# Attention and a two-layer MLP on one core: loads of later chunks with plain token order, K evacuated by two engines, zero fills moved, and product 1 of chunk 0 woven into chunk 1

## The chip, the core and the metric

The kernel runs on one NeuronCore of a Trainium2 chip. Its engines have instruction streams of their own: PE (matrix products and transposes; its weight loads are listed apart as PEld), DVE (vector), ACT (scalar, activation functions), POOL (GpSimd) and SP (which only issues transfers here). The data lie in HBM; SBUF is the working memory and PSUM the memory into which PE writes. The metric is device time in microseconds (us), lower is better. Three runs of the kernel before took 298.2, 299.79 and 300.01 us, the median is 299.79 us.

## The reference

Sliding-window and full attention for 4 batches, 8 heads, 768 tokens and head size 64, followed by two matrix products with a leaky ReLU between them:

```python
scores = scale * q @ k.T                       # per batch and head, 768 x 768
keep_stream = causal & (key < 4 | query - key < 64)
mask = causal if is_retrieval[h] else keep_stream   # heads 0, 2, 6 are retrieval heads
a = softmax(where(mask, scores, -1e9))
x = (a @ v).transpose(0, 2, 1, 3).reshape(3072, 512)
h = x @ w_in                                   # 512 -> 2048
out = maximum(0.01 * h, h) @ w_out             # 2048 -> 512, float32
```

All inputs are float32 in HBM; the products on PE are in bfloat16 with float32 sums.

## The kernel before

The 3072 tokens are eight chunks of 384 (`CH`), two per batch: chunk n is half c = n mod 2 of batch n div 2. Each chunk goes through five steps, and the order of all of them is written out by hand: every engine works through its own list in the order in which the Python code emits the calls, and semaphores make it wait for data.

- **load**: `load_chunk(n)` issues from SP the transfers of k, q and v of chunk n into float32 stage tiles `f` (four of them, used in turn). Token 3p+g of a chunk of q and k goes to partition p, slot g, so that 3 x 64 floats (768 bytes) lie in a row in HBM; one transfer carries all of k or of q. For v, token 128g+p goes to partition p, slot g, in three transfers with rows of 64 floats (256 bytes).
- **cast**: `cast_chunk(n)` turns them into bfloat16 on POOL (for chunk 0 DVE, ACT and POOL share this); `v_shift(n)` copies V, shifted by 64 tokens, into `vb` with two transfers issued from ACT.
- **prep**: `prep_slots(n)` has eight slots, K and Q in turn for four pairs of heads. A slot transposes three 128x128 blocks on PE into PSUM (`pt`, L213) and evacuates them: Q with one copy on DVE (L216), K with two copies of 64 partitions into `kt` (L224 on DVE; in chunks 0 and 1 the second is an ACT copy, L222). Since token 3p+g sits at column p of block g, the copies read PSUM with a step of 128 elements to put the tokens in order. The first four keys of the streaming heads are copied to `ksink` by POOL (L227). Two halves of one PSUM bank take turns as `pt`; in chunks 0 and 1 a third tile, `py`, joins them.
- **attention**: `attention_slots(n)` has units of scores (L296, L331), the exponential on ACT (L301, L336), a mask product on DVE (L305, L340) and, two slots later, the product with V (L251). One unit, `sink_qk`, makes the scores of the four sink keys from `ksink` (L268). A finished pair of heads is scaled on DVE (L357, L359), transposed on PE (L365) and copied by ACT to `xt` (L366). Half c = 1 has 26 slots, half c = 0 has 17 (chunk 0 among them).
- **products**: `in_slots(n)` has 16 ticks of four products (L419) with a leaky ReLU on ACT each (L421); `out_slots(n)` has 16 slots with 48 products (L433), three copies on DVE (L444) and three transfers from SP (L445).

`merge(ms, as_)` puts two lists of slots into one order, spread evenly. In the steady state the prep and attention slots of chunk n+1 are spread over the 32 product slots of chunks n and n-1. The start is different: chunk 0's prep and attention run alone; then come four ticks of product 1 of chunk 0, then prep of chunk 1, then ticks 4 to 11 merged with attention of chunk 1, then 20 ticks in a row (12 of chunk 1, the last four of chunk 0, the last four of chunk 1); then product 2 of chunk 0 merged with prep and attention of chunk 2.

At the very start POOL makes the constant masks, DVE copies some of them together (L117 to L125) and fills the unused halves of `kt` with zeros (L153, L154); after that the two halves of chunk 0's heads are cast and prepared one after the other (L477 to L489).

## Time and profile before

| | |
|---|---|
| median of three runs | 299.79 us |
| time of the profiled execution | 302.08 us |
| its span, first to last instruction | 300.3 us |
| PE busy | 252.7 us, 84% of the span |
| ACT busy | 140.8 us, 47% |
| DVE busy | 130.2 us, 43% |
| POOL busy | 55.6 us, 19% |
| transfers | 32.36 MB, 50760 packets |

How to read it: a row of the table of stages gives a stretch of time, then for each engine its busy time and its number of instructions, the clock that PE was granted (1.00 is full), the busy share of the transfer engines and the rate. A row of the timeline gives start, duration, engine, line, operation, output and input, a count, and in brackets how long the engine had been idle and which instruction or transfer ended that. A queue's name with a q (SPq, ACTq) is the engine that issues transfers; its time is that of the issuing. A row of a group gives count, busy time in us, and the mean of one in ns. PE's products are pipelined, so that the durations of products in a row overlap.

### The profile page before, as it was taken

To read this page: it belongs to the slowest core of one execution; us is meant where nothing else is said; L and a number is where in the kernel's file an instruction comes from. 1 tells how busy PE (TensorE), PEld (TensorE's weight loads), DVE (VectorE), ACT (ScalarE), POOL (GpSimd) and SP (SyncE) were. 2 spreads that over 40 slices of the span, in tenths; PEclk is the share of its full clock that TensorE was granted. 3 is DMA by queue.
4 is the path that set the end of the run, shared out by engine and by line. 5 is a ranking of instruction groups with operands and counts; after the bars stand their busy time and mean duration, and the time that the engine had idled before them with its cause. 6 is when DMAs were issued, how large, how long until landed. Compare 5 with 4: busy or idle time off the path is not lost.

```text
span 300.3 us, 5297 instructions
## 1 busy us (share of the span) xinstructions
PE 252.7 (84%) x2111; PEld 149.9 (50%) x2140; DVE 130.2 (43%) x304; ACT 140.8 (47%) x304; POOL 55.6 (19%) x121
## 2 busy tenths in 40 slices
PE   0266859879789879999999789998998799999994
PEld 0145435555436435665566446664664356655541
DVE  4665552420357563336654552436645623310011
ACT  2164337867305315773366337761565157633300
POOL 8449321000016006000340042000700000000000
PEclk9998577999959999999999999999999999999999
DMA  8899999930100198014901591109511110010011
GB/s 189 230 229 280 208 220 196 285 77 0 35 2 35 37 262 175 2 37 116 281 27 38 115 284 42 37 19 284 119 37 34 56 37 15 23 37 35 35 70 70
DMA packets 50760, 32.36 MB, mean 108 GB/s; under 512 B 26032, under 2 KB 46768, under 8 KB 50736
## 3 DMA queue, kind: packets, MB, share of 16 engines
q1 hardware_dynamic: 45088, 25.04, 31.7%
q0 software_dynamic: 4224, 4.19, 8.2%
q10 hardware_dynamic: 1424, 2.79, 4.3%
q8 instruction: 16, 0.26, 0.4%
q14 instruction: 8, 0.07, 0.1%
HBM read 27.26 MB, written 6.29 MB: 112 GB/s over the span
## 4 chain that ended last, share of the span: by engine, by line
PE 74%; DVE 16%; ACT 4%; issue 3%; POOL 1%; ACTq 0%; DVEq 0%; POOLq 0%
PE ph L419 25%; PE py L433 24%; DVE kt L224 8%; PE pt L213 6%; PE po L251 6%; PE psS L296 4%; PE pt L365 2%; PE psS L433 2%; PE psS L331 2%; DVE xs L359 2%; ACT at L301 1%; DVE o L444 1%; PE psS L268 1%; ACT kt L222 1%; DVE qt L216 1%
## 5 line engine op out<-in xcount | busy, mean ns | idle before, releaser
L419 PE MATMUL ph<-xt,w_in_bf 128*128 128x384 bf16 x512 | 104.5, 333 | 0.1
L421 ACT ACTIVATE g<-ph 128x384 bf16<-128x384 f32 x128 | 62.7, 490 | 83.0 <-PE ph L419 82.4
L433 PE MATMUL py<-w_out_bf,g 128*128 128x512 bf16 x324 | 91.5, 387 | 2.1 <-DVE o L444 0.4
L419 PEld LDWEIGHTS <-w_in_bf 128*128 128x128 bf16 x512 | 46.5, 99 | 29.2 <-issue 4.3
L301 ACT ACTIVATE at<-psS 128x384 bf16<-128x384 f32 x81 | 39.1, 490 | 24.0 <-PE psS L296 23.0
L433 PEld LDWEIGHTS <-g 128*128 128x128 bf16 x384 | 33.8, 98 | 25.2 <-issue 2.8
L224 DVE COPY kt<-pt 64x384 bf16<-64x384 bf16 x54 | 29.9, 554 | 30.7 <-PE pt L213 30.3
L305 DVE TENSOR_TENSOR at<-at,m_caus 128x128 bf16<-128x128 bf16 x72 | 18.1, 279 | 39.6 <-ACT at L301 39.4
L444 DVE COPY o<-py 128x512 f32<-128x512 f32 x21 | 14.5, 689 | 33.4 <-PE py L433 31.4
L296 PE MATMUL psS<-qt,kt 128*128 128x384 bf16 (+2 forms) x105 | 27.7, 305 | 1.2 <-ACT at L301 0.7
L251 PE MATMUL po<-va,at 128*128 128x65 bf16 x252 | 22.7, 199 | 1.6 <-DVE at L305 1.6
L213 PE MATMUL pt<-ident,qb 128*128 128x128 bf16 x84 | 10.0, 231 | 16.7 <-DVE kt L224 12.6
L213 PE MATMUL pt<-ident,kb 128*128 128x128 bf16 x90 | 11.1, 238 | 13.0 <-DVE kb L479 9.0
L340 DVE TENSOR_TENSOR ats<-ats,m_win 128x384 bf16<-128x384 bf16 x40 | 15.6, 393 | 14.4 <-ACT ats L336 14.0
L227 POOL COPY ksink<-kt 64x4 bf16<-64x4 bf16 x20 | 3.7, 183 | 95.6 <-DVE kt L224 89.0
L251 PEld LDWEIGHTS <-at 128*128 128x128 bf16 x252 | 16.8, 102 | 9.0 <-DVE at L305 2.3
L213 PEld LDWEIGHTS <-qb 128*128 128x128 bf16 x96 | 8.8, 108 | 24.7 <-issue 21.4
L216 DVE COPY qt<-pt 128x384 bf16<-128x384 bf16 x28 | 15.6, 556 | 12.3 <-PE pt L213 12.1
L213 PEld LDWEIGHTS <-kb 128*128 128x128 bf16 x96 | 8.7, 107 | 24.4 <-DVE kb L479 11.2
L366 ACT ACTIVATE xt<-pt 128x384 bf16<-128x384 bf16 x30 | 14.7, 488 | 11.6 <-PE pt L365 11.3
L197 POOL CAST kb<-f 128x512 bf16<-128x512 f32 x21 | 12.1, 622 | 40.5 <-PE pt L213 22.5
L336 ACT ACTIVATE ats<-psS 128x384 bf16<-128x384 f32 x37 | 17.8, 488 | 3.0 <-PE psS L331 2.8
(73 smaller groups left out, 229.1 us busy)
## 6 DMA issues: line engine op xcount, KB each, us to landing
f<-in_v_dram SPq DMA_DIRECT2D x24, 256.0 KB, 7.1
out_dram<-o SPq DMA_DIRECT2D x23, 256.0 KB, 2.0
f<-in_k_dram SPq DMA_DIRECT2D x7, 768.0 KB, 6.8
f<-in_q_dram SPq DMA_DIRECT2D x7, 768.0 KB, 8.7
w_in_bf<-in_moe_w_in_dram POOLq DMA_DIRECT2D x4, 512.0 KB, 12.8
w_out_bf<-in_moe_w_out_dram POOLq DMA_DIRECT2D x4, 512.0 KB, 22.1
vb<-va ACTq DMA_DIRECT2D x8, 195.0 KB, 3.5
vb<-va ACTq DMA_DIRECT2D x8, 130.0 KB, 2.9
```

The costliest lines, as they stand in the source:

```text
L213: nc.tensor.transpose(pt[:, g, :], tb[:, g, 2 * p : 2 * p + 2, :], ident[:])
L216: nc.vector.tensor_copy(qts[n][:, p, :].rearrange("p (t g) -> p t g", g=3), pv)
L224: nc.vector.tensor_copy(dst, pv[r])
L251: nc.tensor.matmul(o, lhsT=lhsT, rhs=rhs, start=first, stop=last, skip_group_check=True)
L296: nc.tensor.matmul(s[:, off : off + w], lhsT=kt[i][:, p, hh, 128 * kj : 128 * kj + 128], rhs=qt()[:, p, lo:CH], start=(j == 0), stop=(j == ...
L301: nc.scalar.activation(out=a[:, 0:off], in_=s[:, 0:off], func=ACTF.Exp, scale=SM)
L305: nc.vector.tensor_mul(a[:, off : off + 128], a[:, off : off + 128], m_caus[:])
L336: nc.scalar.activation(out=av_, in_=s[:, 0:CH].rearrange("p (j e f) -> p j e f", j=3, e=2), func=ACTF.Exp, scale=SM)
L419: nc.tensor.matmul(ph[:, 0:CH], lhsT=w_in_bf[:, g, 128 * t : 128 * t + 128], rhs=xts[n][:, g, :], start=(g == 0), stop=(g == KG - 1))
L421: nc.scalar.activation(out=gs[n][:, t, :], in_=ph[:, 0:CH], func=ACTF.Prelu, alpha=0.01)
L433: nc.tensor.matmul(py[n][:], lhsT=gs[n][:, ng, 128 * tt : 128 * tt + 128], rhs=w_out_bf[:, ng, :], start=(ng == 0), stop=(ng == NG - 1))
L444: nc.vector.tensor_copy(o[:], py[n][:])
```

## The change

Five edits:

1. Only chunks 0 and 1 (`WIDE = 2`) keep the 768-byte rows. From chunk 2 on, k and q are loaded like v: token 128g+p to partition p, slot g, in three transfers each with 256-byte rows. The evacuating copies of those chunks read PSUM and write SBUF without a step.
2. The second half of K (hh = 1) is copied by ACT in all chunks, no longer in chunks 0 and 1 alone.
3. The `ksink` copies leave prep and POOL. They are made by DVE inside `sink_qk`, right ahead of the products that read them, in the chunks with c = 0.
4. The zero fills of `kt`, `ksink`, `va` and `vs` of the first pair of buffers come ahead of the masks; DVE's copies of masks (`late_constants`) come after the first half of prep of chunk 0; of chunk 0's V casts ACT takes one of POOL's two; the second block of w_in is requested together with the first; the zero fills of the second pair of buffers go from DVE to POOL and come after the requests for w_out.
5. Product 1 of chunk 0 (all 16 ticks) is merged with prep and attention of chunk 1; the 16 ticks of chunk 1 follow in a row.

```diff
@@ load @@
-        if nm == "v":
+        if nm == "v" or n >= WIDE:
             tv = t.rearrange("p (g h d) -> p g h d", g=3, h=H)
             for g in range(3):
-                nc.sync.dma_start(out=tv[:, g], in_=vr[b, c, :, :, g])
+                nc.sync.dma_start(out=tv[:, g], in_={"q": qr, "k": kr, "v": vr}[nm][b, c, :, :, g])
             return
@@ zero fills @@
     def zeros(i):
-        nc.vector.memset(kt[i][64:128, :, 0, :], 0.0)
-        nc.vector.memset(kt[i][0:64, :, 1, :], 0.0)
+        eng = nc.vector if i == 0 else nc.gpsimd
+        eng.memset(kt[i][64:128, :, 0, :], 0.0)
+        eng.memset(kt[i][0:64, :, 1, :], 0.0)
         nc.gpsimd.memset(ksink[i][:], 0.0)
         nc.gpsimd.memset(va[i][:, :, :, D], 1.0)
         nc.gpsimd.memset(vs[i][:, 0, :], 0.0)
@@ prep @@
-            pv = pt[:, 0:3, :].rearrange("p g t -> p t g")
+            pv = pt[:, 0:3, :]
+            tok = lambda ap: ap.rearrange("p (g t) -> p g t", g=3)
+            if n < WIDE:
+
+                pv = pv.rearrange("p g t -> p t g")
+                tok = lambda ap: ap.rearrange("p (t g) -> p t g", g=3)
             if nm == "q":
-                nc.vector.tensor_copy(qts[n][:, p, :].rearrange("p (t g) -> p t g", g=3), pv)
+                nc.vector.tensor_copy(tok(qts[n][:, p, :]), pv)
                 return
             for hh in range(2):
                 r = slice(64 * hh, 64 * hh + 64)
-                dst = kt[i][r, p, hh, CH * c : CH * c + CH].rearrange("p (t g) -> p t g", g=3)
-                if hh == 1 and n <= 1:
+                dst = tok(kt[i][r, p, hh, CH * c : CH * c + CH])
+                if hh == 1:
                     nc.scalar.activation(out=dst, in_=pv[r], func=ACTF.Copy)
                 else:
                     nc.vector.tensor_copy(dst, pv[r])
-                h = 2 * p + hh
-                if c == 0 and not IS_RETR[h]:
-                    nc.gpsimd.tensor_copy(ksink[i][r, p, 4 * h : 4 * h + NS], kt[i][r, p, hh, 0:NS])
@@ attention @@
         def sink_qk():
+            if c == 0:
+                for h in range(H):
+                    if not IS_RETR[h]:
+                        p, hh = h // 2, h % 2
+                        r = slice(64 * hh, 64 * hh + 64)
+                        nc.vector.tensor_copy(ksink[i][r, p, 4 * h : 4 * h + NS], kt[i][r, p, hh, 0:NS])
             s = score()
@@ start @@
         if half == 0:
-            sv = stage["v", 0].rearrange("p (g h d) -> p g h d", g=3, h=H)
+            late_constants()
             nc.gpsimd.tensor_copy(va[0][:, 0, :, 0:D], sv[:, 0])
             nc.vector.tensor_copy(va[0][:, 1, :, 0:D], sv[:, 1])
-            nc.gpsimd.tensor_copy(va[0][:, 2, :, 0:D], sv[:, 2])
+            nc.scalar.activation(out=va[0][:, 2, :, 0:D], in_=sv[:, 2], func=ACTF.Copy)
             v_shift(0)
             load_w("in", 0)
+            load_w("in", 1)
     for f in attention_slots(0):
         f()
-    zeros(1)
-    cast_chunk(1, between=lambda: [load_w("in", i) for i in (1, 2, 3)])
+    cast_chunk(1, between=lambda: [load_w("in", i) for i in (2, 3)])
     v_shift(1)
     for i in range(4):
         load_w("out", i)
     load_chunk(2)
-    ins0 = in_slots(0)
-    for f in ins0[0:4] + prep_slots(1):
-        f()
-    a1 = attention_slots(1)
-    merge(ins0[4:12], a1)
-    ins1 = in_slots(1)
-    for f in ins1[0:12] + ins0[12:16] + ins1[12:16]:
+    zeros(1)
+    merge(in_slots(0), prep_slots(1) + attention_slots(1))
+    for f in in_slots(1):
         f()
```

Three places in the engines' lists. The first is the head of DVE's list, before:

```order
L117 COPY m_win_96<-m_win 128x256 [waits Pool_49]
L118 COPY m_win_96<-m_caus 128x64
L119 COPY m_win_96<-m_win 128x64
L120 MEMSET m_win_96 4x64 [waits DVE_49]
L125 COPY e_sink<-ident 128x32 [waits Pool_49]
L153 MEMSET kt_111 64x4x384
L154 MEMSET kt_111 64x4x384
L479 CAST kb<-f 128x3x256 [waits DMAHW0_49]
```

and in the changed kernel, whose line numbers are its own (L126, L127 are the zero fills, L496 the K cast, L237 and L229 the copies of K and Q, L115 to L119 the masks):

```order
L126 MEMSET kt_90 64x4x384
L127 MEMSET kt_90 64x4x384
L496 CAST kb<-f 128x3x256 [waits DMAHW0_49]
L237 COPY kt_90<-pt 64x384 [waits PE_49]
L229 COPY qt<-py 128x384 [waits PE_49]
L237 COPY kt_90<-pt 64x384 [waits PE_49,Activation_49]
L229 COPY qt<-pt 128x384 [waits PE_49,Activation_49]
L115 COPY m_win_89<-m_win 128x256 [waits Pool_49]
L116 COPY m_win_89<-m_caus 128x64
L117 COPY m_win_89<-m_win 128x64
L118 MEMSET m_win_89 4x64 [waits DVE_49]
L119 COPY e_sink<-ident 128x32 [waits Pool_49]
```

The zero fills and the first K cast no longer stand behind POOL's masks; the five mask instructions stand between the two halves of chunk 0's prep.

The second place is ACT's list from V's shift of chunk 1 (L188, L189) on, before:

```order
L188 DMA vb_115<-va_113 64x1560 [waits DMAHW3_49,Pool_49]
L189 DMA vb_115<-va_113 64x1560 [waits DMAHW5_49,Pool_49]
L421 ACTIVATE g<-ph 128x384 [waits PE_49] x4
L222 ACTIVATE kt_111<-pt 64x384 [waits DVE_49] x2
L222 ACTIVATE kt_111<-py 64x384 [waits DVE_49]
L222 ACTIVATE kt_111<-pt 64x384 [waits DVE_49]
L301 ACTIVATE at<-psS 128x384 [waits PE_49,Activation_49] x2
```

and in the changed kernel (L235 is the K copy, L437 the leaky ReLU, L317 the exponential):

```order
L196 DMA vb_94<-va_92 64x1560 [waits DMAHW4_49,Pool_49]
L197 DMA vb_94<-va_92 64x1560 [waits DMAHW6_49,Pool_49]
L235 ACTIVATE kt_90<-pt 64x384 [waits DVE_49]
L437 ACTIVATE g<-ph 128x384 [waits PE_49]
L235 ACTIVATE kt_90<-pt 64x384 [waits DVE_49]
L437 ACTIVATE g<-ph 128x384 [waits PE_49]
L235 ACTIVATE kt_90<-py 64x384 [waits DVE_49]
L437 ACTIVATE g<-ph 128x384 [waits PE_49]
L235 ACTIVATE kt_90<-pt 64x384 [waits DVE_49]
L437 ACTIVATE g<-ph 128x384 [waits PE_49]
L317 ACTIVATE at<-psS 128x384 [waits PE_49,Activation_49] x2
```

One tick of product 1 now stands after each pair of prep; ACT's K copies wait for DVE, in both kernels.

The third place is DVE's list at the end of prep of chunk 2 and the start of its attention, before:

```order
L224 COPY kt_112<-pt 64x384 [waits PE_49]
L224 COPY kt_112<-pt 64x384
L444 COPY o<-py 128x512 [waits PE_49]
L216 COPY qt<-pt 128x384 [waits PE_49]
L305 TENSOR_TENSOR at<-at,m_caus 128x128 [waits Activation_49] x2
L305 TENSOR_TENSOR at<-at,m_caus 128x128
L340 TENSOR_TENSOR ats_123<-ats_123,m_win_96 128x3x2x64 [waits Activation_49]
L277 TENSOR_TENSOR vs_118<-psS,m_sink 128x455 [waits PE_49]
```

and in the changed kernel (L460 copies a product, L321 and L356 are the mask products, L280 the sink keys, L293 the sink values):

```order
L237 COPY kt_91<-pt 64x384 [waits PE_49]
L460 COPY o<-py 128x512 [waits PE_49]
L229 COPY qt<-pt 128x384 [waits PE_49,Activation_49]
L321 TENSOR_TENSOR at<-at,m_caus 128x128 [waits Activation_49] x2
L321 TENSOR_TENSOR at<-at,m_caus 128x128
L356 TENSOR_TENSOR ats_102<-ats_102,m_win_89 128x3x2x64 [waits Activation_49]
L280 COPY ksink_99<-kt_91 64x4 [waits Pool_49]
L280 COPY ksink_99<-kt_91 64x4
L280 COPY ksink_99<-kt_91 64x4 [waits DVE_49]
L280 COPY ksink_99<-kt_91 64x4 x2
L293 TENSOR_TENSOR vs_97<-psS,m_sink 128x455 [waits PE_49]
```

One of DVE's two K copies per pair is gone, and five copies of sink keys stand behind a mask product that waits for ACT.

61 lines of the change are left out of this document (34 added, 27 removed).

## The prediction

> **What bounds the kernel now.** I read the page first (chain of waits), then a table of busy time for stages that I cut where PE's timeline changes, then the timeline of single stages, and the transfers last. The chain:
>
> ```profile
> PE 74%; DVE 16%; ACT 4%; issue 3%; POOL 1%; ACTq 0%; DVEq 0%; POOLq 0%
> PE ph L419 25%; PE py L433 24%; DVE kt L224 8%; PE pt L213 6%; PE po L251 6%; PE psS L296 4%; PE pt L365 2%; PE psS L433 2%; PE psS L331 2%; DVE xs L359 2%; ACT at L301 1%; DVE o L444 1%; PE psS L268 1%; ACT kt L222 1%; DVE qt L216 1%
> ```
>
> PE carries three quarters; DVE has 16%, half of it the copy of K. The stages (length, busy time of PE, PEld, DVE, ACT, POOL, PE's clock, share and rate of the transfers) say where PE idles:
>
> ```profile
> 18.00:32.80 14.80, 10.08 (x115) 7.59 (x113) 9.61 (x25) 7.33 (x16) 12.80 (x23) 0.84 1.18 261
> 32.80:44.00 11.20, 7.75 (x43) 4.53 (x41) 5.84 (x9) 3.91 (x8) 1.93 (x4) 0.65 1.20 214
> 44.00:64.00 20.00, 16.20 (x183) 10.58 (x181) 7.46 (x24) 14.11 (x32) 1.85 (x3) 0.88 1.06 219
> 64.00:78.50 14.50, 14.50 (x87) 8.09 (x85) 0.00 (x0) 10.29 (x21) 0.00 (x0) 1.00 0.00 0
> 78.50:89.70 11.20, 8.06 (x41) 3.98 (x40) 6.12 (x12) 0.49 (x1) 1.20 (x6) 0.70 0.11 25
> 138.50:148.70 10.20, 8.93 (x60) 4.87 (x60) 6.89 (x13) 2.45 (x5) 1.52 (x7) 1.00 1.01 256
> 167.40:177.80 10.40, 7.66 (x54) 4.06 (x53) 7.16 (x13) 2.27 (x5) 1.73 (x3) 1.00 0.92 241
> 177.80:201.70 23.90, 23.74 (x237) 14.98 (x239) 8.47 (x26) 16.51 (x37) 3.48 (x6) 1.00 0.19 45
> ```
>
> In order: attention of chunk 0; four ticks and prep of chunk 1; attention 1 with ticks in it; 21 ticks in a row (the last woven one is the first of them); prep of chunk 2; then, from the steady state, prep of chunks 4 and 5 and attention 5. Attention is full there (23.74 of 23.90). What is lost lies in the first 64 us, the 18 us of loading and preparing chunk 0 ahead of this table among them, and in prep, 1.3 us per even and 2.7 per odd chunk. Prep of chunk 5 close up:
>
> ```profile
> 170.41 0.33 PE L213 MATMUL pt<-ident,kb 128*128 128x128 bf16 x3
> 170.57 0.81 PE L419 MATMUL ph<-xt,w_in_bf 128*128 128x384 bf16 x4
> 170.77 1.12 DVE L224 COPY kt<-pt 64x384 bf16<-64x384 bf16 x2 [0.42 <-PE pt L213]
> 171.95 0.33 PE L213 MATMUL pt<-ident,qb 128*128 128x128 bf16 x3 [0.56 <-DVE kt L224]
> 172.31 0.56 DVE L216 COPY qt<-pt 128x384 bf16<-128x384 bf16 x1 [0.42 <-PE pt L213]
> 172.92 0.33 PE L213 MATMUL pt<-ident,kb 128*128 128x128 bf16 x3
> ```
>
> One pair takes 172.92 - 170.41 = 2.51 us: transpose K to copy start 0.36, two copies 1.12, 0.06, transpose Q to copy start 0.36, copy 0.56, 0.05. PE's own work in it is two times 0.16 for transposes (170.41 to 170.57) and two times 0.65 for products (below), 1.6 us, so this chain is the bound.
>
> ```profile
> 33.06 5.12 PE ph L419 x16
> 174.79 0.65 PE py L433 x3
> 54.30 0.66 PE ph L419 x4
> ```
>
> These pieces of the chain of waits also give the price of a tick of four products: 0.66 us, or 5.12/4 = 1.28 in the stage that has a mean clock of 0.65.
>
> **Part 1 and 2: prep from chunk 2 on.** Nothing in the trace shows DVE reading 16-bit PSUM without a step. The nearest rows:
>
> ```profile
> L224 DVE COPY kt<-pt 64x384 bf16<-64x384 bf16 x54 | 29.9, 554 | 30.7 <-PE pt L213 30.3
> L444 DVE COPY o<-py 128x512 f32<-128x512 f32 x21 | 14.5, 689 | 33.4 <-PE py L433 31.4 <-DMA f<-in_v_dram 1.9
> 98.86 0.21 DVE L305 TENSOR_TENSOR at<-at,m_caus 128x128 bf16<-128x128 bf16 x1
> 101.26 0.35 DVE L340 TENSOR_TENSOR ats<-ats,m_win 128x384 bf16<-128x384 bf16 x1
> 10.16 0.48 ACT L222 ACTIVATE kt<-pt 64x384 bf16<-64x384 bf16 x1 [3.65 <-DVE kt L224]
> ```
>
> 384 stepped against 512 float32 elements give (689 - 554)/128 = 1.05 ns per element on 0.15 us fixed. 16-bit rows without a step in SBUF give (0.35 - 0.21)/256 = 0.55 ns. So the copy costs between 0.55 us (PSUM keeps its rate) and 0.15 + 384 x 0.55 = 0.36 us; I take 0.36, since width and step are what differ between the two rates. The Trainium skill (VectorE: DVE Perf Modes, section "The perf-mode tier table") lets a copy out of PSUM go at up to twice the base rate; with the fixed part of the rows that would be 0.15 + 0.20 = 0.35 us, an estimate that no row here shows, and the sum would be the same.
>
> The second half on ACT costs 0.48 us, and it isn't parallel: the ACT row above waited for DVE's copy. The K step becomes 0.36 + 0.36 + 0.03 + 0.48 + 0.06 = 1.29 instead of 1.54; the Q step 0.36 + 0.36 + 0.05 = 0.77 instead of 0.97, but PE's own work then fills that place (0.16 + 0.65 = 0.81). A pair takes 2.10 instead of 2.51, and about 3.5 such intervals count per stage: **-1.5 us** per odd chunk (three, bound 2.7 idle each): -4.5. In even chunks more products are woven in and only 1.3 us are idle: **-1.1** each for chunks 4 and 6: -2.2. Prep of chunk 2 has little beside it and falls to clock 0.70; its chain shrinks the same way from 11.2 us to about 8.5, **-2.5**. With copies at 0.55 the split gains nothing (0.55 + 0.03 + 0.48 against 1.12), so the upper end of all three is 0. ACT has room: 2.27 of 10.40 us busy, and its leaky ReLU comes after the K copy at a time when two `ph` buffers cover it.
>
> **Part 3: sink keys.** POOL made them during prep, hidden. Now PE's sink product waits for five DVE copies, which wait behind a mask product:
>
> ```profile
> 151.94 0.36 DVE L340 TENSOR_TENSOR ats<-ats,m_win 128x384 bf16<-128x384 bf16 x1 [0.38 <-ACT ats L336]
> 151.96 0.60 PE L268 MATMUL psS<-qt,ksink 128*128 128x256 bf16 x4
> 4.10 0.16 DVE L119 COPY m_win<-m_win 128x64 bf16<-128x64 bf16 x1
> ```
>
> Mask product done at 152.30, five copies of up to 0.16 us: PE would start by 153.1, up to 1.1 us late, in a stage where it has no slack, with the following products queued behind it. **+1.0** for each of chunks 0, 2, 4, 6 (between 0, if ACT and DVE run ahead by then, and 1.5): +4.0.
>
> **Part 4: the start.**
>
> ```profile
> 5.67 0.84 ACT L480 ACTIVATE qb<-f 128x768 bf16<-128x768 f32 x1 [3.58 <-DMA f<-in_q_dram]
> 3.50 0.66 DVE m_win L117
> 5.25 1.34 DVE kt L153
> 6.94 1.34 DVE kt L154
> 8.21 0.78 DVE L479 CAST kb<-f 128x768 bf16<-128x768 f32 x1
> 15.40 0.84 ACT L480 ACTIVATE qb<-f 128x768 bf16<-128x768 f32 x1 [3.05 <-DVE kb L479]
> ```
>
> Q of the first half is there at 5.67, K, requested ahead of it, before that; the cast started at 8.21 only because DVE had zeros to fill until 8.28. With the zeros done while the load runs, K's cast starts between 4.5 and 5.7, and Q's cast (5.67 to 6.51) becomes the later one. The first half gains about 3 us or more. Then the masks stand in the way: five instructions that took up to 1.75 us (3.50 to 5.25) beside a busy POOL, 0.8 if each is like the 0.16 row. DVE's V cast gates ACT's transfers and with them the second Q cast (15.40): it comes 1.7 to 2.8 us sooner. I take **-2.8** (bounds -1.0 and -3.6), as POOL is nearly done with masks by then.
>
> **Part 5: the weave.** Before, from 32.85 to 78.5: ticks and prep 11.2, attention 20.0, 21 ticks 14.5. After: four pairs of prep with a tick each. A tick is 1.28 us at half clock and 0.65 at full, two transposes 0.3 to 0.6, so 1.0 to 1.9 us a pair; the chain needs (44.0 - 32.8 - 5.1)/4 = 1.5 a pair: 6 to 8 us and some waits between the two, I take 8 (-3.2). Attention 1 takes 11 ticks instead of 7: 2.6 us more work for PE, which idles 3.8 us there, and four more activations for ACT, about 0.5 each like its copy above; it is 14.11 busy of 20. That it starts at full clock (0.88 in that stage before) is a gain of the same size as what ACT may add, so I take 20.0 (0). In a row stand 17 ticks instead of 21: 14.5 x 17/21 = 11.7 (-2.8). Together **-6.0** (bounds -2, if ACT holds attention 1 back, and -8.5, if the ticks vanish in its gaps). The zero fills of the second buffers leave DVE for POOL, where they stand ahead of the casts of chunk 2, which wait for loads anyway.
>
> **The price of part 1: loads.** q and k of a chunk now come in 256-byte rows like v.
>
> ```profile
> 140.69 6.96 SPq L71 DMA_DIRECT2D f<-in_v_dram  x3
> 28.31 2.97 POOL L88 DMA_DIRECT2D w_out_bf<-in_moe_w_out_dram  x4
> DMA to landing us min/median/max: 18.2/22.1/26.1
> 44.73 0.62 POOL L202 CAST va<-f 128x512 bf16<-128x512 f32 x1 [5.48 <-DMA f<-in_v_dram]
> 51.37 0.62 POOL L202 CAST va<-f 128x512 bf16<-128x512 f32 x1 [6.03 <-DMA f<-in_v_dram]
> 56.91 0.62 POOL L202 CAST va<-f 128x512 bf16<-128x512 f32 x1 [4.93 <-DMA f<-in_v_dram]
> 24.72 12.36 SPq L71 DMA_DIRECT2D f<-in_v_dram  x3
> ```
>
> In the steady state a v piece holds SP 6.96/3 = 2.3 us, nine of them 21 us, so to about 160 instead of 147.7. Casts take under 6 us more; prep of that chunk starts at 167.4: hidden. The stores behind them on SP wait up to 13 us longer, but three `o` buffers cover it. Early on, with the weights loading too, v's pieces of chunk 2 came 6.1 us apart (44.73, 51.37, 56.91). Were all nine so slow, the last would land at 24.7 + 9 x 6.1 = 80. But the last weights, requested by 31.3, land 26.1 us later: after 57 the pieces have the transfers to themselves. Five at 6.1 and four at 2.3 us: 24.7 + 30.5 + 9.2 = 64.4, casts (three of 0.62) to 66.3. Prep of chunk 2 would start at 78.5 - 2.8 + 1.0 - 6.0 = 70.7: hidden, with 4 us to spare. Cost 0.
>
> **Sum.** -2.8 - 6.0 - 2.5 - 4.5 - 2.2 + 4.0 = -14.0 us. The profiled execution took 302.08 us (span 300.3), 0.8% over the median of the runs, 299.79; so 288.1 for a profiled one and **285.8** for a median.
>
> **Rivals.**
> A, DVE reads PSUM no faster: parts 1 and 2 give 0, the rest -2.8 - 6.0 + 4.0 = -4.8: 295.0. For it: every PSUM row here runs at about 1 ns per element. Against it: all of them are either 32-bit or stepped.
> B, the weave is worth little, as attention 1 is held by its own chain of ACT and DVE: part 5 gives -2, the sum is -10: 289.8. For it: PE idles in that stage although ticks are there to be done. With A as well: -0.8, 299.0.
> C, the start becomes load-bound, and this one is slower: chunk 2's nine pieces keep their distance, because chunk 3's pieces press on where the weights end. At 6.6 us each (44.73 to 51.37) the last lands at 24.7 + 59.4 = 84.1, prep starts at 86.0, 15.3 later than forecast, and PE, idle that long, restarts at half clock as at 32.8 (0.65), some 3 us more: 285.8 + 18.3 = 304.1. Every us past a landing at 68.8 counts; it outweighs all gains from 6.1 us per piece on. Against it: the pieces of one queue follow each other, and v's took 2.3 us where nothing else loaded. The Trainium skill (DMA: Bandwidth & Descriptors, section "Specifications") asks for 512 bytes or more per transfer row for full rate, which speaks for this rival; v's rows show what 256 bytes cost here, alone and under load.
>
> **Numbers.** Forecast 0.56, A 0.16, B 0.12, A with B 0.06, C 0.10 (0.06 of it slower by over 1%, the rest about the same). A measurement of this kernel tells about 1% from no change. Faster by over 1% (under 296.8): 0.56 + 0.16 + 0.12 = 0.84; within 1%: 0.10; slower: 0.06. The forecast's own range, with its bounds, is 279 to 291; A stretches it to 296, and beyond lie A with B and C, 0.16, and a little at the lower end.
>
> **What would show it.** Right: K and Q copies of chunks 2 to 7 near 0.36 us on DVE; a pair in odd prep near 2.1 us with PE waiting for ACT's K copy; the first K cast before 5.7 us; PE waiting about 1 us for DVE ahead of the sink product in chunks 0, 2, 4, 6; prep of chunk 2 starting near 71 us at a clock above 0.70. Wrong: copies at 0.55 (A); attention 1 beyond 22 us (B); PE or POOL waiting for loads of q or k past 66 us (C).

## The result, and the profile after

The changed kernel takes **289.62 us** (median of four runs, 288.6 to 290.29) where the kernel before takes 299.9 (298.2 to 300.16): the ratio is 0.966, with a 95% interval of 0.962 to 0.970. Beside the experiments below it was timed again: 289.16 against 300.6, ratio 0.9645 (0.9586 to 0.9704). The forecast was 285.8 with a range of 279 to 296. The profiled execution of the changed kernel took 289.96 us with a span of 288.3, against 302.08 and 300.3 before: 12.1 us less, where the sum said 14.0.

The chain of waits of the changed kernel, by engine and by line:

```profile
PE 75%; DVE 10%; ACT 8%; issue 3%; DMA 1%; ACTq 1%; DVEq 0%
PE py L449 25%; PE ph L435 25%; PE po L261 6%; PE pt L221 6%; PE psS L312 4%; ACT kt L235 4%; DVE kt L237 3%; PE pt L381 2%; PE psS L449 2%; PE psS L347 2%; ACT ats L352 2%; DVE xs L375 2%; PE psS L284 1%; DVE o L460 1%; DMA f<-in_k_dram 1%
```

In the text TensorE is PE of the rows, ScalarE is ACT and GpSimd is POOL. DVE's share fell from 16% to 10%, ScalarE's rose from 4% to 8%, and the copy of K now stands in the chain twice: half on ScalarE (L235), half on DVE (L237). The stages of the changed kernel, cut at the first transposes of K and at the first scores of each chunk (columns as in the prediction's table):

```profile
15.11:31.12 16.01, 10.07 (x114) 7.55 (x113) 9.24 (x30) 7.83 (x17) 9.11 (x15) 0.83 1.24 239
31.12:39.80 8.68, 7.45 (x40) 4.78 (x40) 4.15 (x8) 3.37 (x7) 7.28 (x8) 0.52 1.19 215
39.80:69.48 29.68, 28.45 (x265) 17.98 (x263) 6.85 (x22) 23.47 (x54) 9.29 (x15) 1.00 0.93 173
69.48:80.47 10.99, 8.16 (x41) 4.12 (x40) 2.51 (x8) 2.44 (x5) 0.00 (x0) 0.69 0.11 26
80.47:96.53 16.06, 13.05 (x145) 7.50 (x146) 9.00 (x32) 7.23 (x16) 0.00 (x0) 1.00 0.09 34
96.53:105.13 8.60, 7.20 (x51) 4.05 (x52) 3.31 (x9) 3.91 (x8) 1.55 (x3) 1.00 1.09 207
129.05:138.21 9.16, 8.48 (x61) 4.88 (x61) 3.30 (x10) 4.40 (x9) 2.11 (x4) 1.00 1.15 212
138.21:158.02 19.81, 18.79 (x182) 11.49 (x185) 9.11 (x31) 12.02 (x27) 3.65 (x6) 1.00 0.37 77
158.02:166.93 8.91, 7.20 (x52) 4.05 (x52) 3.43 (x9) 4.17 (x9) 1.61 (x3) 1.00 1.05 200
166.93:190.85 23.92, 23.76 (x238) 15.00 (x239) 8.54 (x25) 16.53 (x37) 4.16 (x7) 1.00 0.40 75
190.85:199.99 9.14, 8.49 (x61) 4.88 (x61) 3.29 (x10) 4.40 (x9) 2.13 (x4) 1.00 1.15 213
199.99:220.05 20.06, 18.78 (x181) 11.50 (x184) 9.20 (x31) 12.12 (x27) 3.42 (x6) 1.00 0.32 75
220.05:228.97 8.92, 7.21 (x52) 4.06 (x52) 3.43 (x9) 4.17 (x9) 0.00 (x0) 1.00 0.28 74
```

In order: attention 0; prep 1 with four ticks; attention 1 and the ticks up to prep 2; prep 2; attention 2; prep 3; prep 4 and attention 4; prep 5 and attention 5; prep 6 and attention 6; prep 7. Three stages of the kernel before, which the prediction did not show, complete the comparison (the same view):

```profile
44.05:78.53 34.48, 30.68 (x265) 18.62 (x264) 7.41 (x24) 24.41 (x53) 1.85 (x3) 0.93 0.61 127
89.70:104.58 14.88, 12.96 (x145) 7.60 (x146) 9.49 (x27) 7.25 (x16) 4.92 (x9) 1.00 0.10 36
148.77:167.45 18.68, 18.44 (x181) 11.60 (x184) 9.08 (x26) 11.94 (x27) 4.56 (x8) 1.00 0.17 45
```

The two profiled executions side by side, in the prediction's own terms (us; from the stage lengths above, those of the prediction and, for chunks 3, 6 and 7 of before, from the same cut, 10.03, 10.25 and 18.69, 10.34):

| term | predicted | measured | how |
|---|---|---|---|
| start, to the first scores | -2.8 | -2.9 | 18.05 to 15.11 |
| weave | -6.0 | -7.3 | prep 1 with ticks 11.20 to 8.68, the rest 34.48 to 29.68 |
| prep 2 | -2.5 | -0.2 | 11.20 to 10.99 |
| odd preps (3, 5, 7) | -4.5 | -4.3 | 10.03, 10.35, 10.34 to 8.60, 8.91, 8.92 |
| even preps (4, 6) | -2.2 | -2.2 | 10.24, 10.25 to 9.16, 9.14 |
| sink keys (attention 0, 2, 4, 6, each stage whole) | +4.0 | +4.9 | 14.80, 14.88, 18.68, 18.69 to 16.01, 16.06, 19.81, 20.06 |
| sum | -14.0 | -12.0 | |

One term is missing almost whole, prep 2. (Of the row of the sink keys, attention 0's +1.2 is not theirs, as the run on the sink keys below shows.) Odd prep close up, chunk 5 of the changed kernel (timeline):

```profile
160.58 0.33 PE L221 MATMUL pt<-ident,kb 128*128 128x128 bf16 x3
...
160.94 0.35 DVE L237 COPY kt<-pt 64x384 bf16<-64x384 bf16 x1 [0.42 <-PE pt L221]
161.33 0.49 ACT L235 ACTIVATE kt<-pt 64x384 bf16<-64x384 bf16 x1 [1.13 <-DVE kt L237]
161.86 0.33 PE L221 MATMUL pt<-ident,qb 128*128 128x128 bf16 x3 [0.31 <-ACT kt L235]
162.29 0.36 DVE L229 COPY qt<-pt 128x384 bf16<-128x384 bf16 x1 [1.00 <-PE pt L221]
162.71 0.33 PE L221 MATMUL pt<-ident,kb 128*128 128x128 bf16 x3
```

A pair takes 162.71 - 160.58 = 2.13 us, forecast 2.10; DVE's copies take 0.35 and 0.36, forecast 0.36. ScalarE's copy starts when DVE's ends, and TensorE waits 0.31 us for it before Q's transposes. Attention 5 is as full as it was (23.76 busy of 23.92).

### The profile page after: what moved, and what is told of

Same layout as the page of the kernel before. It is cut to its first block, busy times and chain, and to the rows that moved or that the text cites. A ratio compares the mean times of both kernels' runs of the same rounds, so it can differ in the third digit from the quotient of the medians.

```text
span 288.3 us, 5327 instructions
## 1 busy us (share of the span) xinstructions
PE 249.1 (86%) x2111; PEld 149.2 (52%) x2140; DVE 105.2 (36%) x298; ACT 152.4 (53%) x329; POOL 59.1 (21%) x102
## 4 chain that ended last, share of the span: by engine, by line
PE 75%; DVE 10%; ACT 8%; issue 3%; DMA 1%; ACTq 1%; DVEq 0%
PE py L449 25%; PE ph L435 25%; PE po L261 6%; PE pt L221 6%; PE psS L312 4%; ACT kt L235 4%; DVE kt L237 3%; PE pt L381 2%; PE psS L449 2%; PE psS L347 2%; ACT ats L352 2%; DVE xs L375 2%; PE psS L284 1%; DVE o L460 1%; DMA f<-in_k_dram 1%
## 5 line engine op out<-in xcount | busy, mean ns | idle before, releaser
L437 ACT ACTIVATE g<-ph 128x384 bf16<-128x384 f32 x128 | 62.9, 492 | 48.6 <-PE ph L435 46.9
L317 ACT ACTIVATE at<-psS 128x384 bf16<-128x384 f32 x81 | 39.2, 492 | 12.4 <-PE psS L312 12.2
L205 POOL CAST kb<-f 128x512 bf16<-128x512 f32 x21 | 12.8, 617 | 109.0 <-DMA f<-in_k_dram 109.0
L321 DVE TENSOR_TENSOR at<-at,m_caus 128x128 bf16<-128x128 bf16 x72 | 15.9, 248 | 40.9 <-ACT at L317 40.8
L235 ACT ACTIVATE kt<-pt 64x384 bf16<-64x384 bf16 x30 | 14.6, 486 | 30.1 <-DVE kt L237 29.8
L460 DVE COPY o<-py 128x512 f32<-128x512 f32 x21 | 14.5, 690 | 36.0 <-PE py L449 34.9
L312 PE MATMUL psS<-qt,kt 128*128 128x384 bf16 (+2 forms) x105 | 26.8, 295 | 0.1
L261 PE MATMUL po<-va,at 128*128 128x65 bf16 x252 | 22.1, 197 | 1.0 <-DVE at L321 1.0
L237 DVE COPY kt<-pt 64x384 bf16<-64x384 bf16 x30 | 11.7, 389 | 26.8 <-PE pt L221 26.8
L356 DVE TENSOR_TENSOR ats<-ats,m_win 128x384 bf16<-128x384 bf16 x40 | 15.1, 377 | 15.2 <-ACT ats L352 14.7
L382 ACT ACTIVATE xt<-pt 128x384 bf16<-128x384 bf16 x30 | 14.7, 489 | 10.8 <-PE pt L381 10.5
L229 DVE COPY qt<-pt 128x384 bf16<-128x384 bf16 x28 | 10.8, 384 | 25.7 <-PE pt L221 25.7
L352 ACT ACTIVATE ats<-psS 128x384 bf16<-128x384 f32 x37 | 17.9, 491 | 2.8 <-PE psS L347 2.8
L205 POOL CAST qb<-f 128x512 bf16<-128x512 f32 x21 | 13.1, 629 | 27.1 <-DMA f<-in_q_dram 20.3
```

What stands on the lines that cost most here:

```text
L205: nc.gpsimd.tensor_copy(tb[:, g], src[:, g])
L235: nc.scalar.activation(out=dst, in_=pv[r], func=ACTF.Copy)
L237: nc.vector.tensor_copy(dst, pv[r])
L261: nc.tensor.matmul(o, lhsT=lhsT, rhs=rhs, start=first, stop=last, skip_group_check=True)
L312: nc.tensor.matmul(s[:, off : off + w], lhsT=kt[i][:, p, hh, 128 * kj : 128 * kj + 128], rhs=qt()[:, p, lo:CH], start=(j == 0), stop=(j == ...
L317: nc.scalar.activation(out=a[:, 0:off], in_=s[:, 0:off], func=ACTF.Exp, scale=SM)
```

## The experiments

Each is an edit of the changed kernel, and each ratio is to the kernel before, run on the same chip. 0.01 of ratio is 3 us.

### Was prep 2 lost to the clock?

The changed kernel once more, without an edit; it is the control for what follows.

> The changed kernel itself beside the other runs of this group, as the kernel before took 298.8 to 302.6 us on one chip and 298.2 to 300.2 on another. Expected ratio to the kernel before 0.966. Also to see whether prep of chunk 2 is 11.0 us long again, at half clock from its fourth us, or 8.5 as in the run without the weave, where the clock stayed at 1.00: theory, the clock decides (11 with a fall, 8.5 without); rival, it is 11 at any clock, because the product pieces between the transposes are longer than in the run without the weave.

Ratio 0.9645 (0.9586 to 0.9704). In this execution prep 2 took 8.52 us and the clock stayed up. Its stage, and two instructions of TensorE's timeline in it:

```profile
70.96:79.48 8.52, 5.60 (x41) 2.96 (x40) 2.69 (x8) 2.44 (x5) 0.00 (x0) 1.00 0.15 33
```

```profile
75.22 0.81 PE L449 MATMUL py<-w_out_bf,g 128*128 128x512 bf16 x3
...
77.19 0.33 PE L221 MATMUL pt<-ident,qb 128*128 128x128 bf16 x3 [0.96 <-ACT kt L235]
```

In the first profile of the same program the same two read:

```profile
73.85 1.49 PE L449 MATMUL py<-w_out_bf,g 128*128 128x512 bf16 x3
...
76.61 0.48 PE L221 MATMUL pt<-ident,qb 128*128 128x128 bf16 x3 [0.96 <-ACT kt L235]
```

Three products take 1.49 instead of 0.81 us, and prep 2 is 10.99 instead of 8.52 long. The program is the same, and so is TensorE's idle time in the stage (2.83 and 2.92 us); its busy time is 8.16 and 5.60. So the difference of 2.5 us is the clock's, and the theory holds. Nine profiles here have no more of TensorE's work in prep 2 than this one: two of them show a fall of the clock in it (10.99 us, and 10.87 in the run on the sink keys), and both of these executions have a mean granted clock of 0.964; the seven without it have 0.973 to 1.0.

The last four of the ticks in a row, moved into prep 2:

```diff
+    ins1, outs0, pr2 = in_slots(1), out_slots(0), prep_slots(2)
-    for f in in_slots(1):
+    for f in ins1[0:12]:
...
-    merge(out_slots(0), prep_slots(2) + attention_slots(2))
+    for j in range(4):
+        for f in (pr2[2 * j], outs0[j], pr2[2 * j + 1], ins1[12 + j]):
+            f()
+    merge(outs0[4:], attention_slots(2))
```

> The changed kernel, but only the last four of the ticks in a row go into prep 2, one behind each pair, with one piece of product 2 between K and Q of a pair. Theory: prep 2 had 8.16 us of TensorE's work in 10.99, half of it at half clock; with four ticks more (2.6 us at full clock) and the clock at 1.00 it takes about 9.2 us like the prep of chunk 4, so 2.6 from the row and 1.8 from prep: 4.4 less than the changed kernel, ratio 0.951. Rival, that the fall of the clock has nothing to do with how full TensorE is: it falls as before, prep 2 takes 13, nothing gained.

Ratio 0.9588 (0.953 to 0.9646), some 1.7 us less than the control instead of 4.4. Prep 2 and attention 2:

```profile
68.43:77.60 9.17, 7.20 (x54) 4.06 (x52) 2.83 (x8) 3.91 (x8) 0.00 (x0) 1.00 0.13 29
77.60:96.33 18.73, 15.57 (x146) 8.86 (x148) 8.65 (x31) 7.71 (x17) 0.00 (x0) 0.91 0.08 30
```

Prep 2 came out as forecast, 9.17 us at full clock. But in this execution the clock fell later, in attention 2 (mean clock 0.91 over 18.73 us), which has little beside it too: 13.05 busy of 15.87 in the control. In this one profile the fall was moved, not removed, so a full prep 2 alone was not enough here.

The next edit fills all of the thin stretch. Product 1 of chunk 1 is woven with product 2 of chunk 0 over prep 2 and attention 2, as the later chunks have it:

```diff
-    for f in in_slots(1):
-        f()
...
-    merge(out_slots(0), prep_slots(2) + attention_slots(2))
+    merge(weave(in_slots(1), out_slots(0)), prep_slots(2) + attention_slots(2))
```

> The changed kernel, with all of product 1 of chunk 1 woven together with product 2 of chunk 0 into prep 2 and attention 2, instead of 16 to 17 ticks in a row ahead of it. In the trace of the changed kernel the ticks in a row took 11.8 us, prep 2 10.99 (8.16 busy, clock 0.69) and attention 2 16.06 (13.05 busy). Chunk 4, which has the same work with the same weave, takes 9.16 + 19.81 = 28.97. Theory: TensorE is dense enough in prep 2 that the clock isn't lowered, the ticks fill its waits and those of attention 2, and from the end of attention 1 (57.7) to prep 3 pass about 29 us instead of 38.8: 9.5 us less, ratio 0.934. Rival: the casts of chunk 2 (V's last ends at 55.1) or the loads of chunk 3 come too late for the earlier start, 4 to 5 us less. Second rival: the clock falls all the same and stays at 0.5 for 7 us, 3 us of the gain lost.

Ratio 0.9441 (0.940 to 0.9483), beside the control's 0.9645: 6.1 us less, not 9.5. Prep 2 and attention 2:

```profile
59.87:69.54 9.67, 8.40 (x61) 4.85 (x60) 3.09 (x9) 4.44 (x10) 3.70 (x6) 1.00 0.53 115
69.54:89.06 19.52, 18.79 (x183) 11.51 (x185) 8.51 (x31) 12.02 (x27) 0.00 (x0) 1.00 0.08 29
```

Together they take 29.2 us, as expected (29), and prep 2 is not held up by loads. What I had too high is the other side. I had let prep 2 start at 57.7, but two ticks, 1.3 us, still stand ahead of it, and attention 1 ended 0.85 later in this execution, so it starts at 59.87; and 2.5 us of the 9.5 were the fall, which only some executions of the changed kernel have. The mean granted clock was 0.974 to 1.0 in all four executions of this kernel, while four of eight of the changed kernel had 0.964 to 0.970; those four took 289.28 to 291.81 us, the other four 288.04 to 289.24. That the four had the fall is read from the mean clock alone, except for the one that was profiled. Why one execution of a program has the fall and another not is not settled by these runs. The Trainium skill (TensorE: Matmul & The Clock Gate, section "Part 1: The HAM clock gate (the "warmup" mystery)") describes a gate that judges TensorE's activity in windows which run freely, not in step with the program; that would make it luck whether a thin stretch of 10 us counts as idle, and agrees with 8.52 and 10.99 us for one program, but no run here could show the windows.

### What the sink keys cost

The copies go back into `one_pair`, behind K's copies, on GpSimd:

```diff
-            if c == 0:
-                for h in range(H):
...
-                        nc.vector.tensor_copy(ksink[i][r, p, 4 * h : 4 * h + NS], kt[i][r, p, hh, 0:NS])
...
+                h = 2 * p + hh
+                if c == 0 and not IS_RETR[h]:
+                    nc.gpsimd.tensor_copy(ksink[i][r, p, 4 * h : 4 * h + NS], kt[i][r, p, hh, 0:NS])
```

> The changed kernel with part 3 alone undone: GpSimd copies the sink keys during prep again. The trace of the changed kernel shows TensorE waiting 0.91, 1.08, 0.73 and about 1.0 us for DVE's five copies ahead of the sink product of chunks 0, 2, 4 and 6. My theory: these waits vanish and nothing takes their place, because the sink product comes at least two slots after the last copy of K: 289.6 - 4.0 = 285.6 us. Rival: GpSimd's small copies stretch prep (they read K's tile right behind the copies and share the way to memory with DVE), prep grows by as much as the waits shrink: 289 to 290. A second rival: the wait was hiding another one (ScalarE's exponentials ahead of the sink product), so that half is left: 287.5.

Ratio 0.9471 (0.9403 to 0.9539), some 5.4 us less than the changed kernel, whose ratio is 0.965. Ahead of it, the changed kernel in attention 4:

```profile
141.76 0.98 DVE L280 COPY ksink<-kt 64x4 bf16<-64x4 bf16 x5
...
142.29 0.83 PE L284 MATMUL psS<-qt,ksink 128*128 128x256 bf16 x4 [0.73 <-DVE ksink L280]
```

and the same stage with the copies back on GpSimd:

```profile
139.09:157.77 18.68, 18.44 (x182) 11.60 (x184) 8.55 (x26) 11.96 (x27) 4.36 (x8) 1.00 0.38 81
```

18.68 is the length that it had before the change to the hundredth, 1.13 less than with the copies on DVE; attention 6 goes from 20.06 to 18.69, and prep 4 is 9.23 instead of 9.16, so that GpSimd's copies cost 0.07 there. In attention 4 and 6 the first theory holds: the waits vanish and nothing takes their place. Attention 2, with 15.13 us, gets back 0.9 (0.7 against the control's 15.87). In attention 0 it doesn't hold: the wait of 0.91 us ahead of the sink product is gone, yet the stage takes 16.27 us, against 16.01 and 16.47 in the two profiles of the changed kernel, as a later wait for DVE's `xs` has grown. So the 1.2 us by which attention 0 grew are not the price of the sink keys; 0.8 of them lie at its end, where the changed kernel goes on with K's transposes of chunk 1, which wait 0.58 us for ScalarE's copy to `xt`, and the kernel before with ticks, which don't.

The traces account for 3.2 to 3.6 us. The rest is within the intervals, and part of it is the clock: three of the four executions have clocks of 0.974 to 0.979 and took 284.45 to 285.06 us, the profiled one has the fall and took 288.49.

### Is the split of K a gain?

```diff
-                if hh == 1:
+                if hh == 1 and n < WIDE:
                     nc.scalar.activation(out=dst, in_=pv[r], func=ACTF.Copy)
```

> The changed kernel, but from chunk 2 on both halves of K leave PSUM on DVE, one after the other, at 0.35 us each, as the split puts ScalarE's 0.49 us behind DVE's 0.35 and not beside it. Theory: the K step shrinks from 0.44 + 0.35 + 0.64 + 0.02 to 0.44 + 0.70, some 0.15 us less wherever TensorE waits for ScalarE's copy (0.31 us in 15 of 16 places of the odd chunks, 0.74 in the first of each), and 0.15 to 0.5 less for the first pair, where ScalarE does a leaky ReLU first: 0.8 per odd chunk, 0.3 per even one, so 289.6 - 3 = 286.6. Rival, that the split is a gain: DVE's extra copy waits behind masks and o copies, 290 to 292.

Ratio 0.9447 (0.940 to 0.9494), some 6 us less than the changed kernel: both halves on DVE are faster. Prep 5 of this kernel:

```profile
157.70 0.33 PE L221 MATMUL pt<-ident,kb 128*128 128x128 bf16 x3
...
158.07 0.72 DVE L237 COPY kt<-pt 64x384 bf16<-64x384 bf16 x2 [0.46 <-PE pt L221]
...
158.85 0.33 PE L221 MATMUL pt<-ident,qb 128*128 128x128 bf16 x3 [0.16 <-DVE kt L237]
...
159.66 0.33 PE L221 MATMUL pt<-ident,kb 128*128 128x128 bf16 x3
```

A pair takes 1.96 us instead of 2.13: two copies in a row, 0.72, are shorter than DVE's and then ScalarE's, 0.35 + 0.04 + 0.49. Odd preps shrink by 0.66 (8.91 to 8.25), even ones by 0.38, prep 2 to 7.23, with the clock up in this execution. By stages that is 2.7 us and 1.3 to 3.8 for prep 2, so the theory was right in kind and low by prep 2.

Could the two halves leave PSUM at the same time? K's halves in tiles of their own:

```diff
-    kt = [one.tile([128, 4, 2, S], BF16, name=f"kt{i}") for i in range(2)]
+    kt = [[one.tile([128, 4, S], BF16, name=f"kt{i}{e}") for e in range(2)] for i in range(2)]
```

> The changed kernel with K's two halves in tiles of their own, so that ScalarE's copy may start with DVE's. Theory: ScalarE waits for DVE only because both write one tile; apart, the K step is 0.44 + 0.49 + 0.02 = 0.95 instead of 1.30, wherever TensorE waits for it (0.31 us in odd chunks, 0.74 in the first pair), so at most 0.31 x 3 + 0.74 less per odd chunk, 0.3 to 0.5 per even one: 289.6 - 5.5 = 284. Rival: what they share is the PSUM bank that they read, ScalarE waits as before, 0.

Ratio 0.9641 (0.9576 to 0.9706), the same as the control; the rival holds. ScalarE still waits for DVE (timeline of prep 5):

```profile
159.44 0.49 ACT L235 ACTIVATE kt<-pt 64x384 bf16<-64x384 bf16 x1 [1.13 <-DVE kt L237]
```

The tile that both wrote was not the reason. What the two copies still share is the PSUM tile that they read (partitions 0 to 63 and 64 to 127 of it). That this is why the built program makes ScalarE wait is likely but not shown, as no run reads the halves from two tiles; nor does a run show whether the chip would let the two copies run side by side.

### The price of the unstepped copies and of the loads

```diff
-    WIDE = 2
+    WIDE = 8
```

> The changed kernel with three-token loads and the stepped copies in all chunks (part 1 undone; the split of K between DVE and ScalarE stays). Theory: DVE's copies go back from 0.35 to 0.55 us, a pair from 2.13 to about 2.5, so 3 x 1.4 in odd chunks and 2 x 0.9 in even ones; prep of chunk 2 loses little (0.3), as half of it runs at half clock and TensorE is the bound there: 289.6 + 6.3 = 295.9. Rival, that the narrow loads cost something that the trace hides in other waits: less than +4, 292 to 293.

Ratio 0.9834 (0.9767 to 0.9901), 5.5 us more than the changed kernel (6.3 expected). Prep 5:

```profile
160.47:170.79 10.32, 7.60 (x53) 4.06 (x52) 4.84 (x9) 4.16 (x9) 1.73 (x3) 1.00 0.92 240
```

That is the length of before, 10.35, to 0.03, although the copies are split here: with stepped copies the split gains nothing, and all of the gain in prep is the unstepped copies'. Prep 2 took 9.79 at full clock, against 8.52 for the changed kernel at full clock: like for like the copies are worth 1.3 us there, not 2.5. The loads in 256-byte rows hold up no prep: in the changed kernel the last cast of chunk 2 is done at 55.1, 14 us ahead of prep 2, and nine pieces hold SP for 10.5 us in the steady state, not the 21 I had bounded it by (K's three, Q's, not shown, and V's of chunk 4):

```profile
54.47 0.62 POOL L210 CAST va<-f 128x512 bf16<-128x512 f32 x1 [0.75 <-DMA f<-in_v_dram]
...
97.56 3.47 SPq L74 DMA_DIRECT2D f<-in_k_dram  x3
...
104.49 3.60 SPq L74 DMA_DIRECT2D f<-in_v_dram  x3
```

Attention 2, 4 and 6 are 0.2 to 0.5 us shorter in the stepped kernel (15.67, 19.52 and 19.63 against the control's 15.87, 19.82 and 20.14). The cause is open; if it is the loads, they cost 1.0 us in all.

### The weave undone

```diff
-    merge(in_slots(0), prep_slots(1) + attention_slots(1))
-    for f in in_slots(1):
-        f()
+    ins0 = in_slots(0)
+    for f in ins0[0:4] + prep_slots(1):
+        f()
+    a1 = attention_slots(1)
+    merge(ins0[4:12], a1)
+    ins1 = in_slots(1)
+    for f in ins1[0:12] + ins0[12:16] + ins1[12:16]:
+        f()
```

> The changed kernel with part 5 undone: four ticks of product 1 ahead of prep 1, eight in attention 1, twenty in a row, the zero fills of the second buffers back ahead of the casts of chunk 1. From the two traces prep 1 with four ticks took 11.15 before and 8.68 after, attention 1 20.00 and 17.90, the ticks in a row 14.53 and 11.78, in all 7.3 us. Theory: 289.6 + 7.3 = 296.9. Rival: part of it came with the earlier start (loads that had landed by then), 293 to 294.

The edit leaves the zero fills of the second buffers where the changed kernel has them. Ratio 0.9812 (0.9773 to 0.9852), 4.9 us more than the changed kernel. From the first scores to prep 2 pass 77.96 - 16.15 = 61.8 us against 70.96 - 16.18 = 54.8 in the control: 7.0 us, as the theory said. For the same 417 products and transposes TensorE is busy 50.2 us of the one stretch and 46.2 of the other, so that 4.0 of the 7.0 us are its slower clock and 3.0 are waits. In this profile and in that of the kernel before, the clock fell in prep 1 and came back 4 to 7 us into attention 1; in all twelve profiles with the weave every tick of attention 1 is at full clock. A tick at the start of attention 1, in the kernel before and in the changed one:

```profile
46.05 1.47 PE L419 MATMUL ph<-xt,w_in_bf 128*128 128x384 bf16 x4
```

```profile
40.13 0.81 PE L435 MATMUL ph<-xt,w_in_bf 128*128 128x384 bf16 x4
```

In this execution the kernel without the weave kept its clock in prep 2:

```profile
77.96:86.48 8.52, 5.60 (x41) 2.96 (x40) 2.68 (x8) 2.43 (x5) 0.00 (x0) 1.00 0.15 33
```

and its four executions have mean clocks of 0.977 to 0.983. So the ratio shows less than 7.0 us presumably because some of the changed kernel's executions have the fall there.

### The start

The old order of the start, with the zeros, the masks and their copies ahead of K's cast and V's third piece on GpSimd:

```diff
-    zeros(0)
     m_caus = one.tile([128, 128], BF16, name="m_caus")
...
-    for a in ats:
-        nc.gpsimd.memset(a[:, :, 1:3, :], 0.0)
...
+    late_constants()
+    zeros(0)
+    for a in ats:
+        nc.gpsimd.memset(a[:, :, 1:3, :], 0.0)
     prep0 = prep_slots(0)
...
         if half == 0:
-            late_constants()
...
-            nc.scalar.activation(out=va[0][:, 2, :, 0:D], in_=sv[:, 2], func=ACTF.Copy)
+            nc.gpsimd.tensor_copy(va[0][:, 2, :, 0:D], sv[:, 2])
```

> The changed kernel with part 4 undone: DVE builds the masks and fills K's zeros ahead of the cast of K, as before, and V's third piece is cast by GpSimd. In the profiled execution of the changed kernel the first scores came at 15.11 us instead of 18.05, 2.9 earlier, but in five other executions of kernels with the same start at 16.15 to 16.18, as K's first load let the cast go 1.3 us later there. Theory: what the reorder is worth is set by that load, 1.9 us in most executions: ratio 0.965 + 0.006 = 0.971. Rival: 2.9 us as in the first trace, 0.975. Second rival: attention 0 absorbs it, as it waits for DVE and the copies of x anyway: 0.965.

Two things about this edit: the change had also moved GpSimd's fills of `ats`, the stream scores, ahead of the sink masks, which its list of five edits doesn't name, and this run moves them back; the second block of w_in and the fills of the second buffers stay as in the changed kernel. Ratio 0.979 (0.9716 to 0.9864), 4.2 us more than the changed kernel, at the upper end or over it. The first scores came at 17.84 instead of 16.18 in the control (1.7), attention 0 took 0.6 more and prep 1 2.3 more (10.07 against 7.79; the other profiles with the weave have 7.8 to 9.0). The last of these is not the order itself. ScalarE's second V shift stood in front of its first K copy and was requested 2.7 us late:

```profile
37.63 0.47 ACTq L194 DMA_DIRECT2D vb<-va  x1
38.15 0.49 ACT L232 ACTIVATE kt<-pt 64x384 bf16<-64x384 bf16 x1 [3.25 <-DMA f<-in_k_dram]
```

By the profile it waited for a load of K, which it doesn't read; presumably the two share a semaphore in this program. In the changed kernel the same two requests follow each other at once. So the worth of part 4 by itself is 1.7 to 2.9 us, and the median of this run overstates it.

The start varies for another reason. DVE's first K cast in the first profile, beside the fill that GpSimd does then:

```profile
4.15 1.77 POOL L150 MEMSET ats<- 128x384 bf16 x4
...
4.30 1.17 DVE L496 CAST kb<-f 128x768 bf16<-128x768 f32 x1
```

and in the control, the same program with the same fill:

```profile
4.26 2.55 DVE L496 CAST kb<-f 128x768 bf16<-128x768 f32 x1
```

To see whether these two stand in each other's way, GpSimd's fills from L150 on were moved behind its V cast, and with them DVE's copy into `e_sink`, which follows one of them:

```diff
-    for a in ats:
-        nc.gpsimd.memset(a[:, :, 1:3, :], 0.0)
...
             load_w("in", 0)
             load_w("in", 1)
+            late_fills()
```

> The changed kernel, with GpSimd's fills of the stream scores and of the sink masks moved from ahead of its V cast to behind it and the weights' first two requests. DVE's first cast of K started at 4.26 to 4.32 in every profiled execution of the new start but took 1.17 us in three of them and 2.55 in one that I read, while GpSimd was writing those fills at 4.15; the old start's cast, alone at 8.21, took 0.78. Theory: DVE's float32 cast and GpSimd's fills stand in each other's way, and which of the two waits is luck; without them the cast takes 0.7 to 0.8, the first transposes start at 5.1 to 5.2 and the first scores near 14.7, if the second cast (at about 11) doesn't meet the fills instead. Rival: the cast is held by the rest of K's load, and it takes 1.2 to 2.5 as before, with the first scores at 15.1 or 16.2.

Ratio 0.9576 (0.9526 to 0.9626), not to be told from the control's. The cast:

```profile
4.35 0.69 DVE L498 CAST kb<-f 128x768 bf16<-128x768 f32 x1
...
9.79 1.46 DVE L115 COPY m_win<-m_win 128x256 bf16<-128x256 bf16 x1
```

0.69 us, and the first transposes start at 5.10. But the fills now meet the mask copies of part 4 (1.46 us instead of 0.22 for the first of them), the second K cast starts at 12.69 instead of 11.07 in the first profile (the copy into `e_sink` now stands right ahead of it, too, and takes 0.64), and the first scores come at 16.16. The theory holds with its condition: the two engines hold each other up, and the fills moved the loss by 5 us without removing it. The Trainium skill (SBUF — State Buffer, section "SBUF: two separate sides") says that these two engines share a pair of ports which one of them locks for a whole instruction, for certain forms of DVE's instructions; that agrees with a cast of 0.69 us that takes 1.17 or 2.55 beside a row of fills. That this cast is of such a form no run here shows.

### The three edits together

Sink keys on GpSimd, both halves of K on DVE, and product 1 of chunk 1 woven with product 2 of chunk 0, by the three diffs above.

> The changed kernel with what the runs so far point to: sink keys copied by GpSimd in prep, both halves of K on DVE from chunk 2 on, and product 1 of chunk 1 woven with product 2 of chunk 0 into prep 2 and attention 2. If the three add up: 5.9 us for the weave, 0.9 + 1.0 + 1.1 + 1.4 = 4.4 for the sink keys, 3 x 0.66 + 3 x 0.37 = 3.1 for the copies, 13.4 in all, 289.2 - 13.4 = 275.8 beside 300.6, ratio 0.918. Rival: they overlap, since the sink waits lie where the weave puts ticks and since DVE carries more in prep; 279 to 281, ratio 0.93.

**275.43 us** beside 300.49, ratio 0.9171 (0.9128 to 0.9213): the three add up in total, and this version beats both kernels, the changed one by 4.9%. Its prep 2 and attention 2:

```profile
59.09:67.88 8.79, 8.37 (x63) 4.86 (x61) 4.53 (x13) 2.50 (x6) 2.02 (x7) 1.00 0.89 166
67.88:86.56 18.68, 18.64 (x185) 11.59 (x184) 9.23 (x26) 11.96 (x27) 4.11 (x8) 1.00 0.08 30
```

TensorE idles 0.42 us in prep 2 and 0.04 in attention 2, where the changed kernel has 2.83 and 3.01 (or 2.92 and 2.82 at full clock).

The same with GpSimd's fills behind all of its work in prep 0:

```diff
+    late_fills()
     for f in attention_slots(0):
         f()
```

> The kernel with the three edits together (275.4 us beside 300.5, ratio 0.917), with the same fills moved behind all of GpSimd's work in prep of chunk 0, where the sink keys' copies hold them back until both casts of K are done. Theory: both casts take 0.7 to 0.8 us in every execution, 0.4 to 1.8 us less at the start and less spread, ratio 0.912 to 0.915. Rival: the fills, done near 19 instead of 8.5, now hold up the first stream scores' exponentials or the sink's mask product, and the gain is given back: 0.917 or more.

275.78 us, ratio 0.9162 (0.9131 to 0.9193): no difference. The first scores came at 14.77 instead of 15.07, but the masks were late (PE's timeline):

```profile
18.29 0.35 PE L266 MATMUL po<-va,at 128*128 128x65 bf16 x3 [2.36 <-DVE at L320]
```

DVE stood before it waiting 2.0 us for the fill of `e_sink`, so the rival holds: the gain at the start was given back in attention 0. The six executions lie closer together, 275.68 to 275.94 instead of 275.0 to 277.24.

## Why the prediction was right or wrong

**The direction, the range and three of six terms were right.** Unstepped copies take 0.35 to 0.36 us (rival A falls), a pair 2.13, the odd preps come to -4.3 for -4.5, the even ones to -2.2. Rival C falls: the last of the loads that prep 2 needs is cast by 55.1 us, earlier than the 66.3 of the forecast.

**The third, the start, was right by luck.** It gave -2.9 for -2.8 in the profiled execution, but -1.9 in six of the other profiles with that start, whose first scores come at 16.15 to 16.18. K's cast started at 4.3 us, even earlier than forecast; that it then takes 1.17 or 2.55 us beside GpSimd's fills, and not 0.78, had no place in the sum.

**The step that failed is prep of chunk 2**: "its chain shrinks the same way from 11.2 us to about 8.5". 8.52 is what it takes at full clock, but 11.2 was a stage in which the clock had fallen to 0.70. The step compared a slowed stage with an undisturbed one. With the fall in both it is 11.20 to 10.99; without it 9.79 to 8.52, where the run with stepped copies stands for the kernel before, which no profile shows without the fall. With the fall the saving is small for two reasons. The second pair wins 0.39 us of waits (0.57 and 0.65 become 0.31 and 0.52), but the first loses 0.35 (0.64 becomes 0.99), as ScalarE issues V's two shifts ahead of its first copy of K. From then on TensorE's own work is slow (1.49 us for three products), and it waits for the copies only once, 0.96 us where it was 1.23. The prediction names the clock of 0.70 in that very sentence and doesn't price it.

**Two terms were mis-sized.** The weave gave 7.3 instead of 6.0. Its row of ticks gave what was forecast (2.8), prep 1 with its ticks took 8.7 for 8, and attention 1 took 17.9 for 20.0. In attention 1 and the row TensorE's idle time falls from 3.80 to 1.23 us, so the four further ticks (2.6 us) did fit into its gaps, and ScalarE's activations cost nothing there. The other 2.2 us are TensorE's busy time, 30.68 to 28.45 for the same 265 products and transposes: the first 4.4 us of attention 1 ran at half clock before. The prediction saw this gain and set it off against a cost of ScalarE's that did not come. Rival B falls with that. The sink keys cost 3.7 us in three stages (1.2, 1.1 and 1.4 in chunks 2, 4 and 6) where 3.0 were forecast, with the mechanism and the place as described; for chunk 0 the forecast had 1.0, and the run without these copies on DVE shows no gain there.

**Carrying a profiled saving to the median was the other failure.** Of the 3.8 us between 285.8 and 289.62 the sum explains 1.9; the other 2.0 are the 0.8% by which the profiled execution of before stood over its median, which I took off the changed kernel too. Its own profile stands only 0.1% above its median. The granted clocks go with this: the profiled execution of before had 0.960, and beside the experiments executions of before with 0.960 took 302.1 to 302.7 us, those with 0.976 or 0.977 298.8 to 300.5. It was one of the former; the two kernels should have been compared at one clock. That the sum itself was only 1.9 us off is in part luck, as the weave's surplus of 1.3 made up for more than half of the 2.3 that prep 2 lacked.

**The split of K was priced rightly and yet is a loss.** DVE and then ScalarE take what the sum said, but I never set that against two unstepped copies on DVE, for which the same estimate gives 0.72, as measured: 0.17 us less per pair.
